# A two-part kernel (recurrent attention and long convolution): x transposes and sixteen projection slices moved into the parameter stage, and a new order of the table rounds

## The chip, the cores and the metric

The kernel runs on one core of a Trainium2 chip. The metric is the device time of one execution in microseconds; the median of several executions counts. TensorE is PE in the profile, VectorE is DVE, ScalarE is ACT, GpSimd is POOL and SyncE is SP. POOL and SP also issue the DMAs.

## What is computed

Two independent results stand side by side in the output. A is an attention over segments of 32 rows with a memory of 8 rows that each segment hands to the next. B is a long convolution whose kernel K is made from state space parameters.

```python
def _A_ref(x, mem0, Wq, Wk, Wv, Wo, seg_len):        # x 2048 x 1024, 32 heads of 128
    for s in range(n_seg):                            # 64 segments
        h = concatenate([mem, x[segment s]])          # 8 + 32 rows
        q, k, v = h @ Wq, h @ Wk, h @ Wv
        p = softmax(where(mask, q @ k.T * scale, -1e9))
        o = (p @ v) @ Wo
        mem = o[:, :M]
        outs.append(o[:, M:])

def _B_ref(u, A_re, A_im, B_re, B_im, C_re, C_im, log_dt, Dskip):   # 1024 channels, 128 states
    dt = exp(log_dt)
    P = exp(dt * A[:, :, None] * arange(L))           # complex A, B, C
    K = einsum('dn,dnl,dn->dl', C, P, dt * B).real
    y = irfft(rfft(pad(u)) * rfft(pad(K)))[:L]
    return y + u * Dskip

out = concatenate([A, B], axis=-1)
```

## The kernel before

The program goes through five stages. Each engine has its own queue and takes its instructions strictly in the order in which the program text issues them, because the kernel sets its schedule by hand.

**Parameter stage (lines 641 to 817).** From A, B, C and dt it works out, in float32, the logarithm of the modulus and the angle of the weights (`modulus`, `angle`), and writes the results to DRAM in three bfloat16 parts, hi, mid and lo (`put3`, tensor `PB`). Beside that run two other pieces of work. `matrices` (L699) makes the sine and cosine matrices `MF` of the transform, in ten steps; a full step is three operations on ACT and four on DVE. `Ahead.transposes` (L84) reads x in 16 blocks of 128 rows over POOL's queue, transposes each with eight PE instructions into one PSUM tile (`pt_x`), and has ACT copy it out in two pieces: `xst`, which SP writes to DRAM as `XTd`, and `xTl`, the last eight rows of each segment, which stays in SBUF. Generators are interleaved by `run`, which takes one step of each in turn. In the version before, the first `run` takes nine steps of the transposes, the second takes the rest with up to three steps a turn.

**Projection slices (`Ahead.projections`, L106).** The last eight rows of every segment don't depend on the memory, so their q, k and v are computed ahead. There are 48 weight pieces of 256 columns, two slices each: 96 slices. A slice is eight matmuls of 128x512 (or 16 of 128x256 for v) into one PSUM tile, and one eviction. Every slice reads all of `xTl`, so none can begin before the last block of x has been copied out. Each weight piece (`wsl`, four buffers) is loaded by SP three pieces ahead. Four slices are issued just ahead of the table rounds (L1110 to L1115).

**Table rounds (L1116 to L1144).** 16 blocks of 64 channels, r = 0 to 15, one a round; f counts from -1 to 16. For each of eight sub-blocks e of a round, PE makes a power tile `pa` (word `X<e>p`) and a phase tile `ptt` (`X<e>t`) from the parameters that POOL loads (`pt`, by `load_par` inside `E0`). ACT takes the exponential of the first (`E<e>`) and shifts the second (`k<e>`); DVE subtracts whole turns (`n<e>`). For each half h of the round, ACT takes the sine (`S`) and the cosine (`C`), DVE the absolute value (`b`, before C), the negation (`w`), and the products imaginary (`gi`) and real (`gr`). PE multiplies them to kernel values (`K0` to `K3`), DVE copies those out (`x0` to `x3`). `pa` has one buffer and `ptt` has two.

Three kinds of side work are put between: projection slices (`P`), transforms of u (`U`, tile `ups`; it needs `MF` and `u_h`) and transposes of `MF` (`M`). Their evictions are words of their own: on ACT p1, p4, A0 and A1, on DVE p0, p2, p3, p5, u0, u1 and m. All of them, and K, share four PSUM tiles. After u0, POOL adds up the parts and writes `Ud`. The list `ORDER` (L600) gives the order of all words within a round; a prime means that the word works on the round before. Side work starts at f = 0; its words ignore the prime.

**Spectra and inverse transforms**, then **part A**, the 64 segments one after the other, which streams weights from DRAM all the time.

Of the kernel before, what the change touches and what calls it, by code (L numbers as in the profile page):

```python
# [16 lines left out]
PSUM = bass.MemoryType.PSUM  # L17
# [568 lines left out]
def bcast_front(ap, n):  # L586
# [10 lines left out]
NF = NP + NN  # L597
NE, NT = NC + NF, NC + NA
PLEN = 4096
ORDER = ("X0p' X0t' P3' b0' w0' C0' b1' P4' p3' C1' gi0' U2' P5' gr0' k0 n0 P0 E0 gr1' p4' X1t X1p p5' k1 X2t P1 E1 n1 p0 A1' k2 w1' X2p n2 "  # L600
         "X3t E2 U3' gi1' p1 X3p k3 X4t P2 E3 n3 k4 u1' X4p X5t p2 E4 U0 n4 k5 X5p n5 K0' E5 A0 X6p X6t E6 M' X7t k6 m' X7p U1 E7 x0' k7 K1' "
         "u0 K2' x1' S0 n6 K3' x2' n7 S1 x3'").split()
ON_ACT = (('p1', 'P', 1), ('p4', 'P', 4), ('A0', 'U', 0), ('A1', 'U', 2))
ON_DVE = (('p0', 'P', 0), ('p2', 'P', 2), ('p3', 'P', 3), ('p5', 'P', 5), ('u0', 'U', 1), ('u1', 'U', 3), ('m', 'M', 0))


def part_b(ctx, tc, u, A_re, A_im, B_re, B_im, C_re, C_im, log_dt, Dskip, out_b, ahead, copies, residents, first_state):
# [6 lines left out]
    v, sc, gp, pe, sy = nc.vector, nc.scalar, nc.gpsimd, nc.tensor, nc.sync  # L614
# [8 lines left out]
    ident = const.tile([128, 128], BF16, name="b_ident")  # L623
# [9 lines left out]
    tabs = ctx1.enter_context(tc.tile_pool(name="b_tab", bufs=1))  # L633
# [5 lines left out]


    with tc.tile_pool(name="b_par", bufs=1) as par, tc.tile_pool(name="b_parh", bufs=2) as parh, tc.tile_pool(name="b_mg", bufs=2) as mg, \
            tc.tile_pool(name="a_prx", bufs=4) as prx, tc.tile_pool(name="a_ppt", bufs=4, space=PSUM) as ppt:
        ldt = par.tile([128, 8], BF16, name="ldt")
        sy.dma_start(out=ldt[:], in_=log_dt.rearrange("(t p) -> p t", p=128))
        nat = {}
# [7 lines left out]
        def f32(name):  # L653
            return par.tile(sh, F32, name=name)

        def put3(x, q, row):
            hi = parh.tile(sh, BF16, name="hi", tag="hi")
            sc.copy(out=hi[:], in_=x[:])
            sy.dma_start(out=PB[q][row].rearrange("t p n -> p t n"), in_=hi[:])
            yield  # L660
            v.tensor_tensor(out=x[:], in0=x[:], in1=hi[:], op=ALU.subtract)
            mid = parh.tile(sh, BF16, name="mid", tag="mid")
            sc.copy(out=mid[:], in_=x[:])
            sy.dma_start(out=PB[q][row + 1].rearrange("t p n -> p t n"), in_=mid[:])
            yield
            lo = parh.tile(sh, BF16, name="lo", tag="lo")
            v.tensor_tensor(out=lo[:], in0=x[:], in1=mid[:], op=ALU.subtract)
            sy.dma_start(out=PB[q][row + 2].rearrange("t p n -> p t n"), in_=lo[:])
            yield

        def run(*gens):
            gens = list(gens)
            while gens:
                for g in list(gens):
                    if next(g, g) is g:
                        gens.remove(g)
# [11 lines left out]
        def some(g, n):  # L688
            for _ in range(n):
                next(g, None)  # L690
                yield
# [7 lines left out]
        def matrices():  # L699

            tms, kMs = {}, {}
            for c in range(0, 20, 2):
                if 4 <= c:
                    tm = tms.pop(c - 4)
                    v.tensor_scalar(out=tm[:].bitcast(I32), in0=tm[:].bitcast(I32), scalar1=0x7FFFFFFF, scalar2=None, op0=ALU.bitwise_and)
                    sc.activation(out=sines(c - 4, 0), in_=columns(tm), func=ACT.Sin, scale=-TWO_PI, bias=hp[:])
                if 2 <= c < 18:
                    tm = tms[c - 2]
                    v.scalar_tensor_tensor(out=tm[:], in0=kMs.pop(c - 2)[:], scalar=MAGIC, in1=tm[:], op0=ALU.subtract, op1=ALU.subtract)
                    sc.activation(out=sines(c - 2, 1), in_=columns(tm), func=ACT.Sin, scale=-TWO_PI)  # L710
                if c < 16:
                    tms[c] = mg.tile([128, 2, 512], F32, name="tm", tag="tm", bufs=4)
                    for i in range(2):
                        v.tensor_scalar(out=tms[c][:, i], in0=colk[:], scalar1=rowl[:, c + i:c + i + 1], scalar2=None, op0=ALU.mult)
                    kMs[c] = mg.tile([128, 2, 512], F32, name="mkM", tag="mkM")
                    sc.activation(out=kMs[c][:], in_=tms[c][:], func=ACT.Identity, bias=magic[:])
                yield

        dt_b = dtb[:].unsqueeze(2).to_broadcast(sh)
        mats = matrices()  # L720
# [23 lines left out]
        v.tensor_scalar(out=low[:], in0=pF[:, 2:3], scalar1=-1.0, scalar2=1.0, op0=ALU.mult, op1=ALU.add)  # L744
        tI = par.tile([128, 8], I32, name="tI")
        gp.iota(tI[:], pattern=[[1, 8]], base=0, channel_multiplier=0)
        own = par.tile([128, 8], F32, name="own")
        v.tensor_copy(out=own[:], in_=tI[:])
        v.tensor_scalar(out=pF[:, 3:4], in0=pF[:, 0:1], scalar1=47.5, scalar2=None, op0=ALU.is_lt)
# [6 lines left out]
        for ts in par_t:  # L756
            for t_ in ts:
                gp.memset(t_[:], 0.0)
        x1, x2, x3, x4, x5, Wr, Wi = (f32(n_) for n_ in ("x1", "x2", "x3", "x4", "x5", "Wr", "Wi"))

        y1, y2 = f32("y1"), f32("y2")
# [12 lines left out]
        def modulus():  # L774

            sc.activation(out=y1[:], in_=Wi[:], func=ACT.Square)
            sc.activation(out=y2[:], in_=Wr[:], func=ACT.Square)
            yield
            v.tensor_tensor(out=x4[:], in0=y1[:], in1=y2[:], op=ALU.add)
            v.tensor_scalar(out=x4[:], in0=x4[:], scalar1=1.0e-37, scalar2=None, op0=ALU.max)  # L780
            sc.activation(out=x4[:], in_=x4[:], func=ACT.Ln)

            sc.activation(out=y1[:], in_=Wr[:], func=ACT.Abs)
            sc.activation(out=y2[:], in_=Wi[:], func=ACT.Abs)
            yield
            v.tensor_scalar(out=x4[:], in0=x4[:], scalar1=0.5, scalar2=None, op0=ALU.mult)
            yield

        def angle():

            v.tensor_tensor(out=x5[:], in0=y1[:], in1=y2[:], op=ALU.max)
            v.tensor_scalar(out=x5[:], in0=x5[:], scalar1=1.0e-37, scalar2=None, op0=ALU.max)
            v.reciprocal(out=x5[:], in_=x5[:])
            v.tensor_tensor(out=x3[:], in0=y1[:], in1=y2[:], op=ALU.min)
            v.tensor_tensor(out=x3[:], in0=x3[:], in1=x5[:], op=ALU.mult)
            sc.activation(out=x3[:], in_=x3[:], func=ACT.Arctan)
            yield
            v.tensor_scalar(out=x3[:], in0=x3[:], scalar1=float(1.0 / TWO_PI), scalar2=None, op0=ALU.mult)
            v.tensor_tensor(out=y1[:], in0=y2[:], in1=y1[:], op=ALU.is_gt)
            v.tensor_scalar(out=y2[:], in0=Wr[:], scalar1=0.0, scalar2=None, op0=ALU.is_lt)  # L800
            v.tensor_scalar(out=Wi[:], in0=Wi[:], scalar1=0.0, scalar2=None, op0=ALU.is_lt)
            yield
            for msk, top in ((y1, 0.25), (y2, 0.5)):
                v.tensor_scalar(out=x5[:], in0=x3[:], scalar1=-2.0, scalar2=top, op0=ALU.mult, op1=ALU.add)
                v.tensor_tensor(out=x5[:], in0=x5[:], in1=msk[:], op=ALU.mult)
                v.tensor_tensor(out=x3[:], in0=x3[:], in1=x5[:], op=ALU.add)
                yield
            v.tensor_scalar(out=Wi[:], in0=Wi[:], scalar1=-2.0, scalar2=1.0, op0=ALU.mult, op1=ALU.add)
            v.tensor_tensor(out=x3[:], in0=x3[:], in1=Wi[:], op=ALU.mult)
            yield  # L810
            yield from put3(x3, 1, 3)

        xs = ahead.transposes(prx, ppt, ident)
        pro = ahead.projections()
        next(pro)
        run(modulus(), put3(x2, 1, 0), put3(x1, 0, 0), some(xs, 9), some(mats, 3))
        run(xs, angle(), xs, put3(x4, 0, 3), xs, mats)


    tmp = ctx1.enter_context(tc.tile_pool(name="b_tmp", bufs=2))  # L820
# [15 lines left out]

    def take(shape, dtype, name):
        return ps_k.tile(shape, dtype, name=name, tag="s")

    def matrices_back():  # L840
        for c in range(16):
# [264 lines left out]
    evict_of = {}  # L1106
    for eng, names in ((sc.copy, ON_ACT), (v.tensor_copy, ON_DVE)):
        for nm, kind, slot in names:
            evict_of[nm] = (kind, slot, eng)
    evict = pro.send((take, tabs))  # L1110
    for i in range(3):
        evict_next = next(pro)
        evict((sc.copy, v.tensor_copy)[i % 2])
        evict = evict_next
    evict(v.tensor_copy)  # L1115
    for f in range(-1, 17):  # L1116
        if f == 15:
            for kind, slot in sorted(k for k in pending if k[0] == "P"):
# [4 lines left out]
        if f == 16:  # L1123
            spectra = [load_u(0), load_u(1)]
        for word in ORDER:
            nm, r = word.rstrip("'"), f - word.endswith("'")
            if f == 16 and word == ORDER[0]:
                s0 = ps_e.tile([128, 2, 512], F32, name="pa", tag="pa")
# [315 lines left out]
```

## Time and profile before

| | |
|---|---|
| median of three runs | 2387.55 us (2379.7 to 2388.32) |
| profiled execution | 2387.04 us, span 2385.3 us |
| parameter stage and first slices | 0 to 92 us |
| first E of the table rounds | 94.74 us |
| first sine (S0) of the first and of the last round | 115.23 and 460.22 us |
| spectra and inverse transforms | to about 717 us |
| part A | about 717 to 2385 us |

The profile is of one execution, with times in microseconds from the start of its span. A line of the timeline gives start, duration, engine, source line, operation, output and inputs, and in brackets how long the engine had been idle and what ended the wait. A table of stretches gives, for each, the busy time of every engine with the number of its instructions, the granted clock of PE, the share of the DMA engines and GB/s.

### The profile page before, as it was taken

What the parts mean: (1) busy time and instruction counts of PE and PEld (TensorE: products, weight loads), DVE (VectorE), ACT (ScalarE), POOL (GpSimd) and SP (SyncE); (2) the same over time, 40 slices, a digit from 0 to 9 for tenths busy, and PEclk for the clock granted to TensorE, in tenths of its full rate; (3) what the DMA queues carried; (4) which work ended last, traced back from release to release, by engine and by line L of the source; (5) the groups of instructions that cost most, each with busy time, mean ns of one, the idle gap of its engine ahead of it and who ended that gap; (6) DMA issues with size and microseconds to landing.
All of it is one profiled execution on the core that took longest, in us unless ns stands there. A gap on an engine that the chain in (4) does not pass through costs nothing.

```text
span 2385.3 us, 78406 instructions
## 1 busy us (share of the span) xinstructions
PE 1993.0 (84%) x33773; PEld 1178.2 (49%) x33798; DVE 1470.6 (62%) x3160; ACT 976.2 (41%) x1599; POOL 361.5 (15%) x623
## 2 busy tenths in 40 slices
PE   1699999779997888788888888888888888878879
PEld 1366665668883444444444444444444444444434
DVE  9599999999973545445455554545555454554540
ACT  6699999713242333233232323333233332323321
POOL 2145354572220000000000000000000000000020
PEclk9999999889997999999999999999999999999999
DMA  6786975684489999999999999999999999999991
GB/s 160 186 243 193 258 217 153 184 266 155 149 289 375 376 386 377 361 376 365 385 381 383 385 379 384 373 390 372 379 382 373 381 386 381 383 361 389 366 383 63
DMA packets 379680, 759.08 MB, mean 318 GB/s; under 512 B 121704, under 2 KB 213000, under 8 KB 377284
## 3 DMA queue, kind: packets, MB, share of 16 engines
q1 hardware_dynamic: 364116, 709.89, 82.7%
q0 software_dynamic: 15216, 44.18, 5.5%
q8 instruction: 264, 4.33, 0.7%
q14 instruction: 84, 0.69, 0.1%
HBM read 699.16 MB, written 67.88 MB: 322 GB/s over the span
## 4 chain that ended last, share of the span: by engine, by line
PE 38%; DMA 32%; DVE 19%; ACT 6%; issue 4%; SPq 1%; DVEq 0%; ACTq 0%; POOL 0%; POOLq 0%
DMA wst<-WD_k 15%; PE acc L349 12%; DMA wst<-WD_o 10%; PE yp L1239 4%; PE hps L1007 4%; DMA wst<-WD_q 3%; PE pp L448 3%; PE pe L571 2%; PE pro L158 2%; DVE nr L1068 2%; DMA wst<-WD_v 2%; PE ups L866 2%; PE tr L360 2%; PE pa L1037 2%; DVE piece L282 1%
## 5 line engine op out<-in xcount | busy, mean ns | idle before, releaser
L349 PEld LDWEIGHTS <-hT 128*32 128x32 bf16 x12352 | 326.2, 97 | 463.0 <-issue 237.5
L349 PE MATMUL acc<-wst,hT 128*32 128x512 bf16 x3072 | 312.2, 390 | 157.9 <-DMA wst<-WD_k 59.1
L349 PE MATMUL acc<-W,hT 128*32 128x512 bf16 x5120 | 399.2, 383 | 0.0
L355 ACT CAST ev<-acc 128x512 bf16<-128x512 f32 x384 | 224.7, 585 | 395.7 <-PE acc L349 390.4
L448 PEld LDWEIGHTS <-oT 128*32 128x32 bf16 x8192 | 204.1, 97 | 118.3 <-issue 92.4
L282 DVE TENSOR_SCALAR piece<-keep 128x256 int32<-128x256 int32 (+1 forms) x640 | 191.3, 363 | 53.0 <-PE pp L448 42.6
L387 DVE TENSOR_REDUCE mx<-sc 128x8 f32<-128x320 f32 x128 | 62.4, 488 | 242.2 <-PE sc L380 242.2
L448 PE MATMUL pp<-W_o,oT 128*32 128x256 bf16 x4096 | 182.4, 276 | 6.0 <-DMA W_o<-in_A_Wo_dram 6.0
L361 DVE COPY KT<-tr 128x512 bf16<-128x512 bf16 x64 | 27.2, 425 | 258.4 <-PE tr L360 258.4
L448 PE MATMUL pp<-wst,oT 128*32 128x256 bf16 x2560 | 128.6, 277 | 41.3 <-DMA wst<-WD_o 32.0
L368 POOL COPY KT<-pk 128x128 bf16<-128x128 bf16 x128 | 37.6, 294 | 798.9 <-PE sc L380 446.7
L349 PE MATMUL acc<-MF,hT 128*32 128x512 bf16 x2048 | 157.9, 382 | 0.0
L361 ACT COPY QT<-tr 128x512 bf16<-128x512 bf16 x128 | 74.9, 585 | 190.0 <-PE tr L360 189.1
L435 ACT CAST oT<-pv 128x512 bf16<-128x512 f32 x128 | 75.0, 586 | 169.8 <-PE pv L421 168.1
L321 POOL COPY hT<-xt 128x192 bf16<-128x192 bf16 x63 | 21.9, 347 | 725.6 <-DMA xt<-XTd 447.8
L158 PE MATMUL pro<-xTl,wsl 128*128 128x512 bf16 x493 | 116.9, 383 | 6.0 <-ACT xTl L102 5.2
L389 ACT ACTIVATE sc<-sc 128x320 f32<-128x320 f32 x128 | 54.0, 422 | 154.6 <-DVE sc L388 149.2
L1007 PEld LDWEIGHTS <-MF 128*128 128x128 bf16 x1024 | 102.7, 101 | 29.6 <-issue 10.5
L1007 PE MATMUL hps<-KT,MF 128*128 128x256 bf16 x720 | 94.7, 284 | 13.6 <-DVE x L1182 10.5
L360 PEld LDWEIGHTS <-ev 128*128 128x128 bf16 x1024 | 57.9, 98 | 96.7 <-issue 67.9
L1239 PE MATMUL yp<-Bt,MI 128*128 128x256 bf16 x680 | 102.8, 273 | 0.8 <-ACT yb L1255 0.8
L360 PE MATMUL tr<-a_ident,ev 128*128 128x128 bf16 x1024 | 101.9, 222 | 0.0
(315 smaller groups left out, 3793.4 us busy)
## 6 DMA issues: line engine op xcount, KB each, us to landing
wst<-WD_o SPq DMA_DIRECT2D x320, 512.0 KB
wst<-WD_k SPq DMA_DIRECT2D x256, 512.0 KB
wst<-WD_q SPq DMA_DIRECT2D x256, 512.0 KB
wst<-WD_v SPq DMA_DIRECT2D x256, 512.0 KB
Ud<-ux POOLq DMA_DIRECT2D x16, 1024.0 KB, 6.1
uq<-Ud SPq DMA_DIRECT2D x32, 512.0 KB
pk<-PKd SPq DMA_DIRECT2D x64, 192.0 KB
wsl<-in_A_Wk_dram SPq DMA_DIRECT2D x16, 512.0 KB
```

What stands on the lines that cost most here:

```text
L158: nc.tensor.matmul(a[:], lhsT=w[:, kc, 128 * j:128 * j + 128], rhs=xTl[:, kc, :, :].rearrange("p s k -> p (s k)"), start=(kc == 0), stop=( ...
L282: nc.vector.tensor_scalar(out=out.bitcast(I32), in0=in_.bitcast(I32), scalar1=0, scalar2=None, op0=ALU.bitwise_or)
L349: nc.tensor.matmul(a[32 * g:32 * g + 32, o_:o_ + rhs.shape[1]], lhsT=hT[:, kc, :], rhs=rhs, start=(kc == 0), stop=(kc == KC - 1), tile_pos ...
L355: nc.scalar.copy(out=q[:], in_=a[:])
L360: nc.tensor.transpose(out=p[:, i, hl, :, :].rearrange("p a b -> p (a b)"), in_=q[:, 128 * hl:128 * hl + 128], identity=ident[:])
L361: eng(out=dst, in_=p[:, i, :, :, :])
L387: nc.vector.tensor_reduce(out=mx[:], in_=sc, axis=AX.X, op=ALU.max)
L389: nc.scalar.activation(out=sc, in_=sc, func=ACT.Exp, scale=scale)
L435: nc.scalar.copy(out=o[:], in_=p[:].rearrange("p a (g q) -> p a g q", g=4))
L448: nc.tensor.matmul(po[32 * qt:32 * qt + 32, :], lhsT=oT[:, h % 4, (h % 16) // 4, :], rhs=columns(w, 1024 * hh + 256 * qt, 256)[0][1], star ...
L1007: pe.matmul(s_[r][half][:, cs, :], lhsT=MF[:, kc, 4 * rr + mc, cs, :], rhs=rhs, start=(i == 0 and mc == 0), stop=(i == 1 and mc == 3), ski ...
L1239: pe.matmul(yp[:, b, :], lhsT=m_[:, b, cs, kc, :], rhs=Bt[:, kc, j, half, c_, :], start=(kc == 0 and cs == 0 and half == 0), stop=(kc == 3 ...
```

## The change

1. The generators of the transposes and of the projections are started earlier, ahead of the computation of `own`. So the first three loads of x stand on POOL's queue ahead of its four memsets. Then twelve steps follow at once: six blocks are transposed and copied out ahead of the parameter arithmetic.
2. The first `run` now takes five steps of the transposes a turn, until all 16 blocks are done, and two steps of `matrices` instead of three.
3. The second `run` interleaves 15 further projection slices with `angle` (two a turn for four turns, then one), after a first one ahead of it: 16 in all, from three PSUM tiles of their own (`a_pps`), all evicted on ACT, each two slices behind. Three steps of `matrices` go with it and the other three follow. The four slices ahead of the table rounds are gone.
4. A round has five slices instead of six (P5 and p5 are gone), and `ORDER` is a new list.

```diff
-ORDER = ("X0p' X0t' P3' b0' w0' C0' b1' P4' p3' C1' gi0' U2' P5' gr0' k0 n0 P0 E0 gr1' p4' X1t X1p p5' k1 X2t P1 E1 n1 p0 A1' k2 w1' X2p n2 "
-         "X3t E2 U3' gi1' p1 X3p k3 X4t P2 E3 n3 k4 u1' X4p X5t p2 E4 U0 n4 k5 X5p n5 K0' E5 A0 X6p X6t E6 M' X7t k6 m' X7p U1 E7 x0' k7 K1' "
-         "u0 K2' x1' S0 n6 K3' x2' n7 S1 x3'").split()
+ORDER = ("k0 X1t X0p' C1' P1' u0' P2' n0 E0 w1' X2t gr1' k1 X1p U2' E1 p1' X2p n1 U3' E2 p2' A1' X3p gi1' U0 E3 k2 X4p X3t M' n2 E4 u1' X4t "
+         "k3 X5p K0' E5 n3 k4 X6p A0 X5t n4 K1' E6 m' k5 X7p X6t E7 n5 K2' x0' k6 x1' X7t n6 P3' x2' k7 S0 K3' p3' n7 P4' x3' S1 w0 b0 P0 "
+         "gi0 p4' C0 b1 X0t U1 p0 gr0").split()
-ON_DVE = (('p0', 'P', 0), ('p2', 'P', 2), ('p3', 'P', 3), ('p5', 'P', 5), ('u0', 'U', 1), ('u1', 'U', 3), ('m', 'M', 0))
+ON_DVE = (('p0', 'P', 0), ('p2', 'P', 2), ('p3', 'P', 3), ('u0', 'U', 1), ('u1', 'U', 3), ('m', 'M', 0))
...
+            tc.tile_pool(name="a_pps", bufs=3, space=PSUM) as pps:
...
         gp.iota(tI[:], pattern=[[1, 8]], base=0, channel_multiplier=0)
+        xs = ahead.transposes(prx, ppt, ident)
+        pro = ahead.projections()
+        next(pro)
+        next(xs)
         own = par.tile([128, 8], F32, name="own")
...
                 gp.memset(t_[:], 0.0)
+        for _ in range(2 * 6):
+            next(xs)
...
-        xs = ahead.transposes(prx, ppt, ident)
-        pro = ahead.projections()
-        next(pro)
-        run(modulus(), put3(x2, 1, 0), put3(x1, 0, 0), some(xs, 9), some(mats, 3))
-        run(xs, angle(), xs, put3(x4, 0, 3), xs, mats)
+        run(modulus(), xs, xs, put3(x2, 1, 0), xs, put3(x1, 0, 0), xs, some(mats, 2), xs)
+        takes = [lambda shape, dtype, name: pps.tile(shape, dtype, name=name, tag="s")]
+        evicts = [pro.send((lambda *a: takes[0](*a), tabs))]
+
+        def projected(n):
+            for _ in range(n):
+                evicts.append(next(pro))
+                if len(evicts) > 2:
+                    evicts.pop(0)(sc.copy)
+                yield
+        first_slices = projected(16 - 1)
+        run(angle(), first_slices, put3(x4, 0, 3), some(first_slices, 4), some(mats, 3))
+        run(mats, first_slices)
+        while evicts:
+            evicts.pop(0)(sc.copy)
...
+    takes[0] = take
...
-    evict = pro.send((take, tabs))
-    for i in range(3):
-        evict_next = next(pro)
-        evict((sc.copy, v.tensor_copy)[i % 2])
-        evict = evict_next
-    evict(v.tensor_copy)
```

More of the change, by code (lines that the diff above doesn't have):

```diff
@@ L641, in part_b @@
     with tc.tile_pool(name="b_par", bufs=1) as par, tc.tile_pool(name="b_parh", bufs=2) as parh, tc.tile_pool(name="b_mg", bufs=2) as mg, \
-            tc.tile_pool(name="a_prx", bufs=4) as prx, tc.tile_pool(name="a_ppt", bufs=4, space=PSUM) as ppt:
+            tc.tile_pool(name="a_prx", bufs=4) as prx, tc.tile_pool(name="a_ppt", bufs=4, space=PSUM) as ppt, \
+            tc.tile_pool(name="a_pps", bufs=3, space=PSUM) as pps:
         ldt = par.tile([128, 8], BF16, name="ldt")
```

## The prediction

> **What bounds the kernel now.** I read the totals first, then the busy time by stage, then the order of instructions inside one table round and at the end of the parameter stage.
>
> ```profile
> PE 1993.0 (84%) x33773; PEld 1178.2 (49%) x33798; DVE 1470.6 (62%) x3160; ACT 976.2 (41%) x1599; POOL 361.5 (15%) x623
> ```
> ```profile
> core 0: us, PE busy (x) PEld busy (x) DVE busy (x) ACT busy (x) POOL busy (x), PEclk, DMA share, GB/s
> 0.00:92.00 92.00, 24.63 (x160) 17.02 (x162) 72.05 (x93) 61.12 (x77) 20.03 (x51) 1.00 0.67 163
> 92.00:115.00 23.00, 18.98 (x114) 10.71 (x114) 10.25 (x17) 14.36 (x22) 1.19 (x2) 1.00 0.92 244
> 115.00:460.00 345.00, 313.28 (x3805) 213.21 (x3821) 322.11 (x490) 319.38 (x390) 163.41 (x192) 0.99 0.73 209
> 717.00:2385.30 1668.30, 1400.67 (x27516) 730.68 (x27519) 838.48 (x2317) 502.31 (x971) 72.68 (x209) 0.99 0.97 367
> ```
>
> The totals name no single bound. By stage: the last 1668 us move 367 GB/s at a DMA share of 0.97; the change touches nothing there. In the parameter stage (0 to 92) DVE is busy 72 us, ACT 61, PE only 25: PE has room for the moved slices. In the table rounds PE, DVE and ACT all stand at 91 to 93%: no engine alone sets the round, so what counts there is the order of waits. One round on ACT, from one S0 to the next:
>
> ```profile
> 207.27 3.39 ACT L1062 ACTIVATE sn<-nr 128x1856 bf16<-128x1856 f32 x2
> 210.66 1.84 ACT L1071 ACTIVATE nr<-nr,hp 128x1856 bf16<-128x1856 f32 x1
> 213.03 1.84 ACT L1071 ACTIVATE nr<-nr,hp 128x1856 bf16<-128x1856 f32 x1 [0.53 <-DVE nr L1068]
> ...
> 215.43 1.28 ACT L1045 ACT_TABLE_LOAD   x1
> 216.72 0.71 ACT L1045 ACTIVATE E<-pa 128x648 bf16<-128x648 f32 x1
> ...
> 223.89 0.71 ACT L1045 ACTIVATE E<-pa 128x648 bf16<-128x648 f32 x1 [0.86 <-PE pa L1037]
> ...
> 228.98 1.28 ACT L1062 ACT_TABLE_LOAD   x1
> 230.27 3.39 ACT L1062 ACTIVATE sn<-nr 128x1856 bf16<-128x1856 f32 x2
> ```
>
> S0 to S0 is 23.00 us (the first S0 is at 115.23, the sixteenth at 460.22: 344.99 / 15). ACT idles about 1.7 of it, in short waits for DVE and PE. And the end of the parameter stage:
>
> ```profile
> 82.65 0.42 ACT L102 COPY xTl<-pt_x 128x256 bf16<-128x256 bf16 x1
> 83.12 0.59 PE L158 MATMUL pro<-xTl,wsl 128*128 128x512 bf16 x1 [5.19 <-ACT xTl L102]
> 83.93 8.22 PE L158 MATMUL pro<-xTl,wsl 128*128 128x512 bf16 x30 [0.22 <-issue]
> 91.98 0.44 PE L1037 MATMUL pa<-RE,pt 128*128 128x324 bf16 x2
> ```
>
> The last eviction of the x transposes ends at 83.1, four slices then hold PE to 92, and only behind them stand the first table matmuls.
>
> **What the Trainium skill says.** "ScalarE: Activation LUTs", What ACT_TABLE_LOAD costs: a load measures about 1283 ns and neighbouring ACTIVATEs overlap by some 93 ns. The trace agrees: every table load takes 1.28, and ACT starts come closer together than durations. So I use slots, start to next start, not durations. "TensorE: Matmul & The Clock Gate", Architectural detail: ACT and DVE take their instructions strictly in order; so one waiting eviction holds all behind it (the 5.19 us above end with ACT's queue). The same page, The HAM clock gate: a cold PE runs at half clock for about 3.4 us. The trace fits: the first four slices took 9.0 us, later ones 1.74 (16 matmuls at 92.62 in 3.47).
>
> **Part 1, the parameter stage.** x's 16 loads (0.54 each on POOL), 128 transposes, 32 ACT copies and 16 XTd writes (0.36 each on SP) stay in number. The first three loads go ahead of POOL's four memsets (4.0 us). The copies of six blocks (6 x 1.1 us in slots) go ahead of the Squares: ACT was idle 9.2 us there, waiting for Wr until 18.45. Hidden.
> The other ten blocks go into the first run. ACT from 18.45: Squares to 21.9 (Wr is late), 2 blocks 2.2, two casts 2.1, one sine step 3.35, table and Ln 2.3, two Abs 2.0, 2 blocks 2.2, two casts 2.1: 38. Then DVE's two lo rows, and the maximum (L791), at 40.48 before, starts at about 39.3, as a sine step has left the space ahead of it. ACT goes on with a table load 1.3, a sine step 3.35 and six blocks 6.6, so xTl is whole at about 49.5 (83.1 before).
> From the maximum to the last lo of x3 it took 40.9 us (40.48 to 81.41). Of DVE's sine work there, 9.9 us, 7.6 stay (three steps of 2.53; the other three now follow): -2.3. The cast hi waited for ACT's queue (3.12 idle on DVE, the cast itself 1.05): -2.1. So lo ends at 39.3 + 36.5 = 76.
> The phase parameters landed about 8.7 us after lo (POOL issued the second pair of loads by 87.8; the shortest landing in the trace is 2.2): ready at 85.
> The 16 slices on PE: 3.4 cold and 15 x 1.74 make 29.5 from 49.5. They have three PSUM tiles, so slice n waits for eviction n-3, which stands in ACT's queue behind sine steps that DVE paces (behind it: the rest of the sine steps and x3's casts; DVE waits for both). Walking cycle by cycle, slices 8 and 9 wait some 1.5 us, and the last ends at 82. Their weight loads stand on SP ahead of PB's rows; the load that stands ahead of mid waits for slice 9, done at 71.5, and mid comes at 74: free. The 16 evictions cost ACT 16 x 0.52.
> ACT's end: eviction 13 at 79.3, then the last sine steps 6.6 and two evictions 1.1: 87. k0 0.6, table 1.28: E0 at 88.9 (94.74 before).
> The first round holds more gain. Before, four slices and a U that waited for u_h (ups at 98.10, 2.03 idle) stood between X0p and X1t (102.6). After, only P1 and P2 (3.5 us) do: E1 at about 90.8, and with the E chain below S0 at 90.8 + 10.9 = 101.7, where it was 115.23. **-13.5 us.**
>
> **Part 2, the rounds.** Leaving: eight matmuls (1.74 us) of PE and one DVE eviction (slot 0.60; p5). ACT loses nothing. I walk the new order with slots of the old round (us from S0). DVE: after S0, 1.78; w0 0.80, b0 1.53, gi0 1.52, b1 1.57 (7.2), p0 0.60, gr0 1.52, u0 1.20, n0 0.63: 11.15. ACT meanwhile: S1, p4, C0 at 4.2, k0, C1 at 7.22 (b1), table, E0 at 10.26. X2t stands on PE ahead of X1p and waits for n0, so X1p is at 11.4 and E1, 0.48 later as before, at 11.9. E2, E3, E4 follow at 1.24, the closest spacing in the trace. X4t waits for n2 (w1 0.27, gr1 1.52, n1 0.55, p2 0.60, gi1 1.52, n2 0.63: 16.2), E5 at 17.0, with k4 and A0 E6 at 18.6, E7 19.84; X7t waits for n5 (20.5), k7 21.0 to 21.65, table 1.28: S0 at **22.9**. PE: P3, P4, P0, P1, P2 are done by 9.2 and idle until 11.2; no slice is in the way. So the round goes from waits on PE to a DVE chain of nearly the same length: 15 x (22.9 - 23.0) = **-1.5 us**. The walk leaves out waits that I can't see and may be off by 0.25 a round either way, +-4 us.
>
> **Part 3, the way out.** From the last S0 to the last gi took 13.7 us (460.22 to 473.96). In the new order DVE has w0, b0, gi0, b1, p0, gr0, the KN negation 1.65, u0, w1, gr1, gi1: with the 1.78 it comes to 15.5. **+1.8 us.** The last five slices on PE lie under that chain. Part A's 1668 us: unchanged.
>
> **Sum:** -13.5 - 1.5 + 1.8 = -13.2, against the profiled span of 2385.3. That execution took 2387.04, near the median of 2387.55 (the three runs lie between 2379.7 and 2388.32). 2387.55 - 13.2 = 2374.3; I say **2374**.
>
> **The rivals.**
> (B) The rounds shrink by what leaves DVE or more: 0.7 a round, to 22.3. For: ACT's 21.3 busy is the only floor above that, and PE has 1.7 us more room. Against: the walk. -13.5 - 10.5 + 1.8: 2365.
> (C) Slower: the parameter loads. In the new order u0 stands ahead of E0, so POOL's adds for it (7.9 us from u0, to 17.2), the 1 MB Ud write and then the four loads of the next round's parameters are queued: issued at 18 to 20.4, not right after Ud at the head of the round as before (191.46, with the next X0t some 16 us later). X0t is due at 27.1. Landings in the trace are 2.2 to 8.3 us, median 5.8. There are 1.3 us of room behind X0t (k0 isn't due before 6), so it decides from a landing of about 8.2 us; each us above costs 15, and from 9.1 the change loses. At 9.8: +1.6 x 15 - 13.2: 2398. Against: it needs every round above the longest landing seen.
> (D) The early gain is half lost: the XTd writes keep the four xst tiles (six blocks in a row on ACT, 1.1 us apart), or ACT's queue keeps PE's slices later than I walked. For: ACT would be some 70 us busy of 87. 6 us later: 2380.
>
> **Chances.** Forecast (A) 0.54, B 0.20, C 0.08, D 0.18. About 0.5% (12 us, below 2375.6) is what a measurement of this kernel can tell from no change. A, 2374 +-5, lies on that line: 0.33 faster, 0.21 same. B is faster. C: 0.06 slower, 0.02 same. D: 0.15 same, 0.03 faster. Sum: faster 0.56, same 0.38, slower 0.06. The range 2361 to 2387 takes in A with the walk's error on both sides, D, and most of B; it leaves out C.
>
> **What would show it.** Right: slices from about 50 us on PE, first E near 89, first S0 near 102, and 22.9 between S0s with E1 released by n0 on DVE (X2t). Part 1 is wrong if the first S0 comes after 106; part 2 if the spacing is below 22.6 (B) or above 23.2; C shows as X0t waiting for a DMA of pt. It is all wrong if the last stage's length moves by more than some us.

## The result

The changed kernel takes 2420.35 us (median of 4, 2408.2 to 2424.42) where the kernel before takes 2387.41 (median of 4, 2379.7 to 2388.32): a ratio of 1.0137, 95% interval 1.0092 to 1.0181. It is 1.4% slower. The profiled execution of it took 2416.76 us, with a span of 2415.0.

The two spans divide at three events: the first S0, the last S0, and the first weight load of part A.

| | before | after | difference | predicted |
|---|---|---|---|---|
| start to first S0 | 115.23 | 111.41 | -3.8 | -13.5 |
| first to last S0, 15 rounds | 344.99 | 369.62 | +24.6 | -1.5 |
| last S0 to part A | 257.1 | 263.0 | +5.9 | +1.8 |
| part A | 1668.0 | 1671.0 | +3.0 | 0 |
| span | 2385.3 | 2415.0 | +29.7 | -13.2 |

The rounds bring nearly all of the loss. The parameter stage brings a gain, but a quarter of the one that was expected. Part A, whose instructions nobody touched, has a length of its own in every execution: over the eleven kernels profiled here it lies between 1654 and 1677 us. So a single time can't tell a few microseconds, and the readings below rest on the three events, with the times beside them.

The totals of the page after:

```profile
PE 2037.6 (84%) x33769; PEld 1190.8 (49%) x33798; DVE 1478.3 (61%) x3145; ACT 983.7 (41%) x1614; POOL 362.9 (15%) x623
```

The instructions of PE did not grow, yet its busy time did, by 44.6 us. The table of stretches shows where (columns as before: length, busy time and instructions of PE, its weight loads, DVE, ACT and POOL, then PE's clock, the DMA share and GB/s):

```profile
core 0: us, PE busy (x) PEld busy (x) DVE busy (x) ACT busy (x) POOL busy (x), PEclk, DMA share, GB/s
0.00:92.00 92.00, 47.91 (x257) 26.76 (x261) 73.13 (x92) 65.92 (x88) 19.43 (x51) 0.98 0.81 204
...
111.00:481.00 370.00, 327.82 (x3671) 212.92 (x3691) 326.83 (x480) 319.84 (x391) 160.28 (x184) 0.92 0.61 179
744.00:2415.00 1671.00, 1405.62 (x27513) 729.56 (x27518) 839.20 (x2317) 502.89 (x971) 73.17 (x209) 0.98 0.97 366
```

In the rounds DVE is busy for longer than before (326.8 against 322.1 us) although an eviction a round has left it, and PE's granted clock is 0.92 where it was 0.99. ACT's busy time is what it was. So two things have to be explained: DVE's instructions became longer, and PE runs cold. One round on ACT, from one S0 to the next, by the timeline:

```profile
235.48 3.39 ACT L1081 ACTIVATE sn<-nr 128x1856 bf16<-128x1856 f32 x2
...
244.70 0.71 ACT L1064 ACTIVATE E<-pa 128x648 bf16<-128x648 f32 x1
...
248.41 0.71 ACT L1064 ACTIVATE E<-pa 128x648 bf16<-128x648 f32 x1
...
251.97 0.71 ACT L1064 ACTIVATE E<-pa 128x648 bf16<-128x648 f32 x1 [2.32 <-DVE gi L1039]
...
257.88 1.28 ACT L1081 ACT_TABLE_LOAD   x1
259.17 3.39 ACT L1081 ACTIVATE sn<-nr 128x1856 bf16<-128x1856 f32 x2
```

E0 to E3 (244.70 to 248.41) follow each other without a gap. Then E4 waits 2.32 us for gi1 of the round before, which is still reading E. The round of the kernel before that the prediction shows has no wait of that length. What DVE did in those microseconds:

```profile
245.41 2.19 DVE L1038 TENSOR_TENSOR gr<-E,nr 128x1824 bf16<-128x1824 bf16 x1
247.52 1.09 DVE L1039 TENSOR_TENSOR gr<-E,nr 128x768 bf16<-128x768 bf16 x1
...
249.68 1.18 DVE L1038 TENSOR_TENSOR gi<-E,sn 128x1824 bf16<-128x1824 bf16 x1
250.79 1.09 DVE L1039 TENSOR_TENSOR gi<-E,wn 128x768 bf16<-128x768 bf16 x1
```

and POOL beside it:

```profile
244.01 1.26 POOL L901 TENSOR_TENSOR ux<-us 128x512 f32<-128x512 f32 x1 [12.60 <-DVE us L896]
245.24 1.38 POOL L902 TENSOR_TENSOR ux<-us 128x512 f32<-128x512 f32 x1
246.58 4.87 POOL L904 TENSOR_TENSOR ux<-us 128x256 f32<-128x256 f32 x4
```

The two pieces of gr1 take 2.19 and 1.09 us. The same two pieces of gr0, some 4 us earlier and before POOL starts, take 1.11 and 0.57. POOL's six adds run from 244.01 to 251.45, and just the DVE instructions inside that stretch whose inputs all lie in SBUF (w1, gr1 and gi1) are longer than elsewhere. The order before had placed u0 so that the adds ran beside b0, w0 and b1. There the first w of a round and b are the long ones, and gr1 and the second w, later in the same round, are short:

```profile
185.91 4.67 POOL L885 TENSOR_TENSOR ux<-us 128x256 f32<-128x256 f32 x4
...
187.54 0.88 DVE L1075 TENSOR_SCALAR wn<-sn 128x768 bf16<-128x768 bf16 x1
188.34 1.65 DVE L1068 TENSOR_SCALAR nr<-nr 128x1856 int32<-128x1856 int32 x1
...
194.28 1.12 DVE L1019 TENSOR_TENSOR gr<-E,nr 128x1824 bf16<-128x1824 bf16 x1
...
197.54 0.35 DVE L1075 TENSOR_SCALAR wn<-sn 128x768 bf16<-128x768 bf16 x1
```

The new order has u0 ahead of E0, and the adds run beside w1, gr1 and gi1.

On PE the lateness ends in a long wait in each round. The two largest sums of PE's waits between the first and the last S0 (engine and line, what it waited for, total, times, longest), and what follows such a wait:

```profile
PE ptt L1050 <- DVE nr L1076: 35.9, 27, 2.2
PE pa L1056 <- ACT E L1064: 4.0, 16, 0.4
```

```profile
224.10:227.50 3.40, 1.35 (x13) 0.75 (x11) 3.40 (x5) 1.09 (x3) 3.09 (x4) 1.00 0.93 200
...
210.10:235.50 25.40, 22.69 (x256) 16.16 (x249) 21.78 (x32) 21.35 (x28) 10.82 (x12) 0.87 0.83 218
235.50:259.20 23.70, 20.88 (x288) 15.57 (x289) 22.15 (x33) 21.20 (x27) 10.83 (x12) 1.00 0.63 181
```

```profile
227.09 0.36 PE L1050 MATMUL ptt<-RT,pt 128*128 128x464 bf16 x1 [2.05 <-DVE nr L1076]
227.35 0.62 PE L1056 MATMUL pa<-RE,pt 128*128 128x324 bf16 x2
228.88 0.72 PE L1056 MATMUL pa<-RE,pt 128*128 128x324 bf16 x2
```

X4t waits 2.05 us for n2, which stands behind gr1 and gi1 on DVE. In the 3.4 us up to 227.5, PE is busy for 1.35. From there its clock is halved for 6.8 us: a pair of pa matmuls takes 0.72 where it takes 0.44 at full clock. A round in which that happens takes 24.5 to 26.6 us; the rounds at full clock take 23.7 (the last, 22.6). Over all 370 us the clock of 0.92 means 370 x 0.08 / 0.5, some 59 us at half speed.

Nine rounds have such a cold stretch and five have the wait and stay warm. The trace's record of the clock tells most of the difference. All its changes lie on one grid with a step of 3.41 us, and the nine cold stretches start at the end of grid windows in which PE was busy for 1.2 to 2.0 us. In the five warm rounds the least busy window has 1.5 to 2.3 us, mostly because the wait lies across two windows: at 251.4 it is divided into windows with 2.45 and 2.14 us of work. A warm round of 23.69 us is 0.2 us shorter than seven windows, so the wait slides along the grid: 2.04, 1.83, 1.62 us of work in three successive rounds, and after the third the clock is halved. The two ranges overlap between 1.5 and 2.0, so this is no sharp limit.

### The profile page after: what moved, and what is told of

Same layout as the page of the kernel before. It is cut to its first block, busy times and chain, and to the rows that moved or that the text cites. A ratio compares the mean times of both kernels' runs of the same rounds, so it can differ in the third digit from the quotient of the medians.

```text
span 2415.0 us, 78423 instructions
## 1 busy us (share of the span) xinstructions
PE 2037.6 (84%) x33769; PEld 1190.8 (49%) x33798; DVE 1478.3 (61%) x3145; ACT 983.7 (41%) x1614; POOL 362.9 (15%) x623
## 4 chain that ended last, share of the span: by engine, by line
DMA 37%; PE 27%; DVE 18%; issue 8%; ACT 7%; POOL 1%; SPq 1%; ACTq 0%; DVEq 0%; POOLq 0%
DMA wst<-WD_k 15%; PE acc L349 12%; DMA wst<-WD_o 11%; PE pp L448 3%; DMA wst<-WD_v 3%; DMA wst<-WD_q 2%; PE pe L571 2%; DMA out_dram<-uu 2%; PE tr L360 2%; DVE gr L1038 2%; DMA KT<-Kd 1%; DVE piece L282 1%; DVE nr L1087 1%; DVE gi L1038 1%; ACT ev L355 1%
## 5 line engine op out<-in xcount | busy, mean ns | idle before, releaser
L1064 ACT ACTIVATE E<-pa 128x648 bf16<-128x648 f32 x128 | 91.3, 713 | 44.0 <-DVE gi L1039 32.4
L1026 PE MATMUL hps<-KT,MF 128*128 128x256 bf16 x720 | 94.8, 284 | 14.1 <-DVE x L1195 11.1
```

The lines of the kernel that those rows point to most:

```text
L1026: pe.matmul(s_[r][half][:, cs, :], lhsT=MF[:, kc, 4 * rr + mc, cs, :], rhs=rhs, start=(i == 0 and mc == 0), stop=(i == 1 and mc == 3), ski ...
L1064: sc.activation(out=T["E", r, e // 4][:, lo:lo + 8 * NE].rearrange("p (i c) -> p i c", i=2), in_=T.pop(("p", r, e))[:, :, 0:4 * NE], func= ...
```

## The experiments

Theory PORT: DVE and POOL hinder each other whenever POOL's adds run beside DVE instructions that read SBUF; the new order puts the adds beside the chain that sets the round. Theory ORDER: the new order is longer by its own dependencies, whatever POOL does. A second question is how much of the loss is PE's clock, and a third where the gain at the start went.

### The parameter stage alone

```diff
-ORDER = ("k0 X1t X0p' C1' P1' u0' P2' n0 E0 ...
+ORDER = ("X0p' X0t' P3' b0' w0' C0' b1' P4' ...      # the list of before
-ON_DVE = (... ('p3', 'P', 3), ('u0', 'U', 1), ...
+ON_DVE = (... ('p3', 'P', 3), ('p5', 'P', 5), ('u0', 'U', 1), ...
```

> The changed parameter stage with the old order of the rounds (six slices a round, of which 80 are left, so they end in round 13). Theory PORT (POOL's adds for u now run beside DVE's products gr1 and gi1 and slow them, and the wait that follows lets PE's clock fall): the old order puts the adds under b0, w0 and b1 again, so S0 to S0 is 23.0 in rounds 0 to 12, and what is left of the change is its early gain of about 4 us: 2381 to 2386. Theory COLD (PE's clock falls because the rounds hold less PE work, whatever POOL does): rounds 13 to 15, which have no slices, become 1 to 2 us longer each and eat the gain: 2386 to 2392. If the parameter stage itself were what loses, it would stay above 2395.

Measured: 2388.14 us (median of 16) against 2389.97, ratio 0.9993 (0.9970 to 1.0017): no change. Most rounds are 23.0 long (mean 23.12), with one of 26.0 in which PE waited 2.8 us for a weight piece. The loss is in the new order. The time lies in COLD's range and above PORT's, but not for COLD's reason: the last three rounds take 22.9, 22.1 and 22.7 and are no longer than the others. What is missing is the gain: the first S0 comes at 119.1, later than before. With the old order PE has ahead of X1t two slices that wait 3.04 us for ACT, and then the rounds' first transform of u, which waits for its input; how much each of the two costs was not tested. The transform:

```profile
101.88 1.05 PE L885 MATMUL ups<-u_h,MF 128*128 128x256 bf16 x8 [2.71 <-DMA u_h<-in_B_u_dram]
```

### The adds taken out

```diff
-x_ = up.tile([128, 4, 2, DQ], F32, name="ux", tag="ux")
-gp.tensor_tensor(out=x_[:, 0], in0=e_[:, 0], in1=o_[:, 0], op=ALU.add)
...
-gp.dma_start(out=Ud[kc, dq], in_=x_[:])
+for i, t_ in enumerate((e_, o_)):
+    gp.dma_start(out=Ud[kc, dq][:, 2 * i:2 * i + 2], in_=t_[:])
```

> The changed kernel without POOL's six adds for each fourth U; the two tiles of partial sums are written to Ud as they are, so the last step of u's transform is left out. PORT: gr1 takes 1.11 and 0.57 us again (2.19 and 1.09 now), S0 to S0 is 22.8 to 23.1, PE stays at full clock in nearly all rounds, total about 2396. ORDER (the new order's own chain of waits is longer than the old one's, POOL or not): gr1 gets faster, but S0 to S0 stays at 23.6 or above. COLD: PE has the same work as now and still falls to half clock in about half of the rounds; S0 to S0 24 or more on average.

This kernel leaves out the last step of u's transform, so it prices the adds and doesn't replace them. Measured: 2372.48 us (one run), mean spacing 21.56 us, PE's clock 1.00 in the rounds. The groups of DVE in the rounds (count, busy time, mean in ns, idle time before):

```profile
L1083 DVE TENSOR_SCALAR nr<-nr 128x1856 int32<-128x1856 int32 x14 | 15.6, 1115 | 0.0
...
L1034 DVE TENSOR_TENSOR gr<-E,nr 128x1824 bf16<-128x1824 bf16 x14 | 15.6, 1115 | 0.0
L1035 DVE TENSOR_TENSOR gr<-E,nr 128x768 bf16<-128x768 bf16 x14 | 7.9, 566 | 0.0
```

With nothing but POOL's adds gone, the round falls by 3.1 us and every gr is back at 1.115 and 0.566. ORDER falls: without the adds the new order is not the longer one (the old order without them follows below). It is also shorter than was expected here and than the 22.9 that the prediction walked, which points at the slots of the walk.

### PE kept busy in the wait

```diff
-for kc in range(4):
+for kc in range(16):
     for cs in range(2):
-        pe.transpose(out=mt[:, cs, kc, :], in_=MF[:, kc, c, cs, :], identity=ident[:])
+        pe.transpose(out=mt[:, cs, kc % 4, :], in_=MF[:, kc % 4, c, cs, :], identity=ident[:])
```

> The changed kernel with the eight transposes of each M issued four times over (the same values are written again), 1.4 us more PE work a round, just ahead of the phase matmul that waits 2 us for n2. PORT: the wait for n2 is still there (gr1 at 2.19), the filler lies in it, PE keeps its full clock, and all rounds take the 23.7 us of the undisturbed ones now: about 14 us less than now, 2403 to 2408. COLD: the same 14 us, and gr1's duration has nothing to do with it. ORDER: no gain, or slower by up to 1.4 us a round, 2420 to 2440.

Measured: 2400.26 us (one run), mean spacing 23.63. More work on PE made the round shorter. The stretch of the rounds, and gr1 in one of them:

```profile
112.00:468.00 356.00, 325.27 (x4046) 222.81 (x4064) 327.89 (x482) 319.20 (x392) 162.64 (x187) 1.00 0.64 187
```

```profile
240.93 2.19 DVE L1038 TENSOR_TENSOR gr<-E,nr 128x1824 bf16<-128x1824 bf16 x1
243.04 1.10 DVE L1039 TENSOR_TENSOR gr<-E,nr 128x768 bf16<-128x768 bf16 x1
```

The clock is 1.00 and gr1 is as slow as in the changed kernel. So the two parts come apart: of 24.64 - 21.56 = 3.08 us a round, the clock is 24.64 - 23.63 = 1.01 and the collision of DVE and POOL 23.63 - 21.56 = 2.07. The second is near what DVE's instructions lost in the round shown above: gr1 1.07 + 0.52, gi1 0.07 + 0.52, w1 (0.51 against 0.35) 0.16, together 2.34. The waits in which PE cools come from the collision too: the runs without it, before and below, keep a clock of 1.00.

### u0 later in the round

```diff
-... k0 X1t X0p' C1' P1' u0' P2' n0 E0 ... k5 X7p X6t E7 ... X7t n6 P3' ... X0t U1 p0 gr0
+... k0 X1t X0p' C1' P1' P2' n0 E0 ... k5 X7p U1 X6t E7 ... X7t n6 u0 P3' ... X0t p0 gr0
```

> The changed kernel with U1 and its eviction u0 moved from the round's turn to its end: U1 behind X7p, u0 behind n6, so POOL's adds start about at S0 and lie beside w0, b0, gi0 and b1 as they lay before. PORT: gr1 1.11, b0 and b1 about 1.6 (1.12 now), S0 to S0 23.0 to 23.3, full PE clock in most rounds, 2392 to 2400. ORDER: S0 to S0 stays at 23.6 or above, 2410 or more.

Measured: 2430.39 us (median of 4), ratio 1.0167 (1.0112 to 1.0222) to the kernel before, mean spacing 25.83 and PE's clock 0.93. The rounds are longer than the changed kernel's; the intervals of the two ratios overlap. PORT's forecast failed, and the numbers are those that ORDER gave. The adds did leave gr1 (1.12 again) and fell on w0, b0 and gi0:

```profile
243.91 0.74 DVE L1092 TENSOR_SCALAR wn<-sn 128x768 bf16<-128x768 bf16 x1 [0.33 <-ACT sn L1079]
244.57 1.65 DVE L1085 TENSOR_SCALAR nr<-nr 128x1856 int32<-128x1856 int32 x1
246.14 1.64 DVE L1036 TENSOR_TENSOR gi<-E,sn 128x1824 bf16<-128x1824 bf16 x1
247.71 1.09 DVE L1037 TENSOR_TENSOR gi<-E,wn 128x768 bf16<-128x768 bf16 x1
```

b1 comes later by that, C1 waits 1.24 us for it, X2t then waits 2.85 us for DVE, and PE cools there. So the conflict followed the adds to their new place, but the run doesn't price it, since the move lengthened other waits as well; by its time alone it can't tell PORT from ORDER.

### The adds held back behind gi1

The adds stay; POOL first copies two elements that gi1 has written, and so starts only when gi1 is done. Then DVE does n, u, m, p and x, each of which takes an input from PSUM.

```diff
-gp.tensor_tensor(out=x_[:, 0], in0=e_[:, 0], in1=o_[:, 0], op=ALU.add)
...
+def add(e_=e_, o_=o_, x_=x_, kc=kc, dq=dq):
+    gp.tensor_tensor(out=x_[:, 0], in0=e_[:, 0], in1=o_[:, 0], op=ALU.add)
...
+adds.append(add)
...
 products(r, h, "gi", windows(T.pop(("s", r, h))), T.pop(("w", r, h))[:])
+if h == 1 and adds:
+    mark = tmp.tile([128, 2], BF16, name="mark", tag="mark", bufs=1)
+    gp.tensor_copy(out=mark[:], in_=T["gi", r, h][:, NE - 2:NE])
+    while adds:
+        adds.pop(0)()
...
```

> The changed kernel with its full computation, in which POOL holds its adds for u back until DVE has written gi1, so that they run beside n, u, m, x and p, which read PSUM. Theory PORT: gr1 back to 1.12 + 0.57 us, gi1 to 1.11 + 1.09 at most, b at 1.1, spacing 21.5 to 21.9, time 2368 to 2378, faster than before. The adds in their new place may slow the small DVE copies beside them by a few tenths. Theory ORDER: spacing 23.6 or more and a time near 2400 or above. If Ud's later writes were in the way (the rest of u's path), X0t would wait for the DMA of pt.

Measured: 2367.76 us (median of 8, 2365.01 to 2372.3) against 2392.98, ratio 0.9899 (0.9869 to 0.9930), mean spacing 21.56. DVE's gr1 and gi1, then POOL, in one round:

```profile
249.11 1.11 DVE L1042 TENSOR_TENSOR gr<-E,nr 128x1824 bf16<-128x1824 bf16 x1
250.15 0.57 DVE L1043 TENSOR_TENSOR gr<-E,nr 128x768 bf16<-128x768 bf16 x1
...
251.78 1.11 DVE L1042 TENSOR_TENSOR gi<-E,sn 128x1824 bf16<-128x1824 bf16 x1
```

```profile
253.44 0.19 POOL L1104 COPY mark<-gi 128x2 bf16<-128x2 bf16 x1 [12.49 <-DVE gi L1043]
253.58 1.27 POOL L903 TENSOR_TENSOR ux<-us 128x512 f32<-128x512 f32 x1
254.82 1.27 POOL L904 TENSOR_TENSOR ux<-us 128x512 f32<-128x512 f32 x1
256.06 2.78 POOL L906 TENSOR_TENSOR ux<-us 128x256 f32<-128x256 f32 x4
```

The full computation has the same 21.56 us a round as the one without adds. The four small adds take 2.78 us instead of 4.87: POOL had lost about as much as DVE. E4 no longer waits, and from E0 to the next table load it takes 11.02 us where the changed kernel took 13.18. The clock is 1.00, without a filler: in this order the cooling was a consequence of the collision.

### The kernel before, without the adds and with the adds held back

The first of these two makes the edit of the run without adds, the second that of the run with the adds held back, both on the kernel before.

> The kernel before without the six adds of POOL for each half of u's transform; the partial sums are written to Ud by two DMAs instead, so the last step of u's transform is left out. A control for the run without adds of the changed kernel (spacing of the S0s 21.56 us). Theory PORT (DVE and POOL slow each other whenever both read two SBUF operands): in the kernel before the adds slow b0, b1 and w0; without them b is 1.1 us instead of 1.6 and w0 0.36 instead of 0.88, and the spacing falls from 23.0 to 22.0 to 22.5, a time near 2375. If it falls to 21.5 as well, six against five slices in a round is worth nothing without the conflict; if it stays at 23.0, what five slices and their order are worth is the whole 1.4 us. Theory ORDER (the new order's own chain is what is long): says nothing on this run, it stays near 23.0.

> The kernel before with nothing changed but the place of POOL's adds: held back until DVE has written gi1, full computation. It tells what of the gain of the last two versions is the change's own and what is the adds' place alone. Theory PORT: b0, b1 back at 1.12 us and w0 at 0.36, spacing 22.0 to 22.2 as without the adds (22.07), 15 x 0.93 = 14 us less than before, ratio to before 0.993 to 0.996; then the change, with the adds in the same place, is worth 15 x 0.54 = 8 us in the rounds besides the first S0 (11 us earlier in the version with the later weight loads). Rival: held back in this order, the adds collide with the next round's us buffers (three of them), DVE's u waits for POOL, and the spacing stays at 22.6 or more.

Measured: without adds 2370.99 us (one run; the last step of u's transform is left out here too), spacing 22.07. With the adds held back 2375.27 (median of 6, 2369.77 to 2378.19) against 2385.01, ratio 0.9959 (0.9939 to 0.9980), spacing 22.08. The row of b in the rounds, first in the kernel before as it was, then with the adds held back:

```profile
L1068 DVE TENSOR_SCALAR nr<-nr 128x1856 int32<-128x1856 int32 x12 | 19.4, 1618 | 0.0
```

```profile
L1072 DVE TENSOR_SCALAR nr<-nr 128x1856 int32<-128x1856 int32 x14 | 15.8, 1127 | 1.7 <-ACT sn L1066 1.7
```

The kernel before paid for the same collision, and less for it. The spacings side by side:

| spacing of S0, us | adds where u0 puts them | adds held back | no adds |
|---|---|---|---|
| order before, six slices | 23.00 | 22.08 | 22.07 |
| new order, five slices | 24.64 | 21.56 | 21.56 |

The new order with its five slices is worth 0.52 us a round (its two parts, the order and the slice that left, were not separated), and it turned a collision of 0.92 us into one of 3.08. With the adds held back in both, the change is a gain: the last S0 comes at 433.07 against 446.11. The ratios, 0.9899 and 0.9959, have intervals that don't overlap, but each is taken against its own runs of the kernel before (2392.98 and 2385.01), and the two medians lie only 7.5 us apart.

### The first weight loads later on SP

```diff
 pro = ahead.projections()
-next(pro)
 next(xs)
...
 for _ in range(2 * 6):
     next(xs)
+next(pro)
```

> The changed kernel with the three first loads of projection weights (SP) behind XTd's writes of the first six blocks instead of ahead of them; rounds as changed. Theory: the 7.30 us for which the fifth block's xst eviction waits for the XTd write go, the Squares start near 19 to 20 instead of 26.3, the maximum near 39.5 to 40.5 instead of 44.4, and the first S0 near 106 instead of 111.4; rounds as in the changed kernel (24 to 25). Rival: the slices' weight loads come later and ACT's queue is still behind, first S0 stays within 2 us of 111.4.

In the changed kernel the fifth block's copy on ACT waits for the buffer `xst`, and SP shows why:

```profile
23.49 0.80 ACT L101 COPY xst<-pt_x 128x768 bf16<-128x768 bf16 x1 [7.30 <-DMA XTd<-xst]
```

```profile
8.90 5.70 SPq L116 DMA_DIRECT2D wsl<-in_A_Wk_dram  x3
14.72 14.66 SPq L103 DMA_DIRECT2D XTd<-xst  x7
```

`projections` was started ahead of the transposes, and its three weight loads hold SP until 14.6. Only then the first XTd write is issued, and `xst` has four buffers. With the loads behind six blocks' writes, the same copy:

```profile
16.62 0.80 ACT L101 COPY xst<-pt_x 128x768 bf16<-128x768 bf16 x1 [1.02 <-DMA XTd<-xst]
```

Measured: 2406.11 us (one run), first S0 at 106.53 instead of 111.41, the rounds as in the changed kernel (24.64). The Squares start at 19.88 instead of 26.29 and the maximum at 39.59 instead of 44.42, so the wait cost 4.8 us on the way to S0. The first S0 itself isn't that exact: over the five kernels with the changed kernel's start and a form of the new order it lies between 109.7 and 112.3, over the two with the later loads at 104.1 and 106.5.

### Both edits on the changed kernel

> The two edits together (adds behind gi1; first weight loads behind six blocks' XTd writes), full computation. Theory PORT and the late start together: spacing 21.5 to 21.9, first S0 near 106, 2363 to 2373, faster than both kernels. If only the spacing follows: the same as with the adds held back alone. Theory ORDER: near 2395.

Measured: 2358.31 us (median of 4, 2352.06 to 2363.31) against 2392.98, ratio 0.9874 (0.9828 to 0.9920). First S0 at 104.09, spacing 21.53. The median is 5 us below the range that was expected. The rounds:

```profile
104.00:427.00 323.00, 302.23 (x3681) 201.42 (x3680) 294.63 (x480) 317.75 (x391) 128.62 (x195) 1.00 0.73 207
```

Against the kernel before, the span of its profile has -11.1 to the first S0, -22.1 in the rounds, +2.9 to part A and -4.7 in part A, which no edit touches. The first three, -30.3, are the version's own. It beats both kernels.

## Why the prediction was wrong

The forecast was 2374, with a chance of 0.56 for faster and 0.06 for slower. It is 2420, outside the range of 2361 to 2387. Between the forecast of the span and the profiled one lie 42.9 us: 26.1 in the rounds, 9.7 at the start, 4.1 on the way out and 3.0 in part A.

**Part 2 is the step that failed**, in its words "I walk the new order with slots of the old round". It is also the largest of the four terms. A slot holds what runs beside it. The old round's slots for b0 (1.53), b1 (1.57) and w0 (0.80) were measured with POOL's adds beside them; those for w1, gr1 and gi1 were measured with POOL idle. In the new order it is the other way round, and the walk had both wrong. It used 0.80 for w0 and 0.27 for w1, two instructions of one shape, and did not ask why. To E1 it is 10.45 us from S0 (235.48 to 245.93), where the walk had 11.9: b0, b1 and w0 are shorter by 0.5 each. From E1 to the next S0 it is 13.24, where the walk had 11.0: the collision. The errors partly cancel (-1.45 + 2.24 = +0.8, so 23.7 for a round at full clock); the clock adds 1.0 to the mean. With the adds held back, E1 comes 10.46 after S0 and the next S0 11.07 after that: then the walk's second half holds to 0.1, and its first half differs by the three slots alone.

The prediction did place the adds in time. Rival C has them "7.9 us from u0, to 17.2". But it asked only what was queued behind them on POOL, and not what they share with the engine beside them. The page "SBUF — State Buffer" of the Trainium skill, section Who interferes with whom, says that a DVE instruction with two SBUF inputs contends with a GpSimd instruction that reads SBUF, and that a tensor_scalar in a mode that uses both ports does too. The trace agrees on who is hit: gr and gi (two SBUF inputs), b and w (tensor_scalar) are stretched, n, u, x, m and p, with an input from PSUM, are not (n 0.63 beside the adds, as elsewhere). The page also says that the later of the two is fully blocked until the instruction of the other is over. The trace agrees in each single record, though both engines' instructions get longer: they block each other in turn, and the blocked time is inside the recorded duration, not in an idle time with a named wait. In the round shown (us; "left" is what the other engine's instruction still had to run when this one started; the trace holds the four small adds one by one, where the view above has one line, x4):

| instruction | start | took | alone | longer by | left |
|---|---|---|---|---|---|
| gr1, first piece | 245.41 | 2.19 | 1.11 | 1.08 | 1.21 |
| first small add | 246.58 | 1.61 | 0.72 | 0.89 | 1.02 |
| gr1, second piece | 247.52 | 1.09 | 0.57 | 0.52 | 0.66 |
| second small add | 248.15 | 1.05 | 0.72 | 0.33 | 0.47 |
| third small add | 249.16 | 0.73 | 0.72 | 0.01 | 0 |
| gi1, first piece | 249.68 | 1.18 | 1.11 | 0.07 | 0.20 |
| fourth small add | 249.84 | 1.61 | 0.72 | 0.89 | 1.02 |
| gi1, second piece | 250.79 | 1.09 | 0.57 | 0.52 | 0.66 |

Each that had something left ahead of it is longer by that, less some 0.13 us. Between 111 and 475 us the changed kernel has 126 such overlaps of the adds with b, w, gr or gi, and this holds for every one to within 0.02 us; the other 138 of these instructions, which start with nothing of the other engine's left, take their usual time to within 0.01. In the round shown DVE loses 2.3 us in all and POOL 2.2 (its six adds take 7.44 from the first start to the last end, and 5.26 held back).

**PE's clock was left out of part 2.** The page "TensorE: Matmul & The Clock Gate", section HAM oscillation — how this bites in real kernels, warns of gaps on PE above some 3.4 us, and its section What's actually happening gives an idle window of about that length as the cause of the half clock. The half clock in steps of 3.4 us agrees. The length of the gap doesn't: here waits of 2.05 us, in a window of 3.4 with 1.35 us of work, were followed by it (1.01 us a round, by the run with the filler). Not every such wait was; where it fell on the grid decided in most rounds, as shown above. This reading of the grid comes from the traces; no run was made to test it.

**Part 1** said first S0 at 101.7; it came at 111.41, past the 106 named as its limit. Its own steps, with the values of the changed kernel and of the run with the weight loads later:

| | predicted | after | loads later |
|---|---|---|---|
| maximum starts | 39.3 | 44.42 | 39.59 |
| xTl whole, first slice | 49.5 | 53.58 | 49.47 |
| last lo ends | 76 | 81.0 | 76.2 |
| last slice ends | 82 | 88.9 | 84.0 |
| first ptt (parameters landed) | 85 | 90.10 | 86.82 |
| first E0 | 88.9 | 96.14 | 91.30 |
| E1 | 90.8 | 100.15 | 95.28 |
| first S0 | 101.7 | 111.41 | 106.53 |

The term that failed first is "The copies of six blocks go ahead of the Squares ... Hidden." They weren't, because of the XTd writes behind SP's weight loads. This is rival D's first mechanism (four xst tiles), but its cause was a DMA queue that the change moves past another piece of work, and that I had counted for the later weight loads only. With the wait gone the walk holds to 0.3 us for the first three rows. The rest, 4.8 us, comes at the end (in the run with both edits half of it, 2.4 us, is left): the last slices, the parameters and E0 are some 2 us late, and then E1. It has P1 and P2 ahead of it on PE, priced at 3.5 us at full clock and without a wait. In the changed kernel:

```profile
90.10 0.55 PE L1050 MATMUL ptt<-RT,pt 128*128 128x464 bf16 x2 [1.24 <-DMA pt<-PB]
90.49 0.44 PE L1056 MATMUL pa<-RE,pt 128*128 128x324 bf16 x2
94.33 5.32 PE L145 MATMUL pro<-wsl,xTl 128*128 128x256 bf16 x32 [3.40 <-ACT kst L167]
```

They wait for ACT to evict the last of the 16 slices and then run partly cold, 5.32 us.

**Part 3** had +1.8 from the last S0 to the last gi. It is 19.20 us where it was 13.73, +5.5. The last round collides as well: its gr1 takes 2.18 + 1.09, its gi1 1.63 + 1.09. With both edits it is 15.94, +2.2, near the forecast, though there too one group of adds falls on b0, gi0 and b1 (1.64 to 1.65 each).

**The rivals.** B (the rounds shrink by 0.7 to 22.3, by what leaves DVE) comes near once the adds are held back in both kernels: 0.52. The 21.56 lies below B's 22.3 because holding the adds back took another 0.92 off the old round. C forecast a slower kernel for a reason that isn't seen: in the rounds PE waits for no parameter load at all. The 2398 that it gave was nearer than the forecast by accident. No rival named a shared resource.

## What to carry to other kernels

When an order is walked with durations of the old trace, write beside each what ran on the other engines at that moment, above all DVE and POOL on SBUF; a move that changes the neighbours changes the duration. So compare the shortest and the longest duration of the same shape in the trace before: w took from 0.34 to 0.89 there, and that was the warning. It need not show: b took 1.55 to 1.65 all 32 times, always beside the adds, and its 1.12 was seen only after they had moved. And follow every generator or block that is started earlier through each queue it issues on: here three loads ahead of the writes cost some 4.8 us.

## What the runs showed of the hardware that was not expected

- POOL's adds (two SBUF inputs, float32) and DVE's products lengthen each other at the same time: gr 1.11 to 2.19 and 0.57 to 1.09, four adds 2.78 to 4.87. The int32 tensor_scalar b goes from 1.12 to 1.65 and w from 0.35 to 0.88 beside them, although they have one tensor input.
- The price isn't fixed by the instruction, but by what is left of the other engine's instruction at its start, less some 0.13 us (126 overlaps of the changed kernel, to within 0.02): gi's first piece took 1.64 where an add had 0.67 us left, and 1.18 where one had 0.20.
- Waits of some 2 us within a stretch in which PE is busy for nearly nine tenths were followed by half clock for 3.4 to 10.2 us. In the changed kernel's rounds this came after grid windows of 3.41 us with 1.2 to 2.0 us of PE work, and not after those with 2.04 or more. More work on PE in the wait made the kernel faster, 2400 us (one run) against 2420.
